# Loading the first contraction quarter of a gated FFN tile by tile, the second half of x in four transposes, and two warm-up matmuls fewer

## Chip, cores, metric

One core of a Trainium2 chip. The time of a kernel is the device time of one execution in microseconds (us); lower is better. Compared are ratios of runs made in the same rounds on the same chip. A single core's execution that is within 1.5% of the fastest of its kernel counts as fast.

## The reference

Tokens 1024, model width D = 1024, hidden width F = 3584, everything in bf16:

```python
# x (32, 32, 1024), w_gate and w_up (1024, 3584), w_down (3584, 1024)
def reference(x, w_gate, w_up, w_down):
    return (gelu_tanh(x @ w_gate) * (x @ w_up)) @ w_down
```

## The kernel before

The contraction over D runs in 8 tiles of 128 (`DT`), two to a quarter (`KQ = 2`). x is wanted with D on the partitions, so it is fetched by DMA transposes; tokens come in two halves of 512 (`NB`). F is worked through in seven chunks of 512 columns. All loads but one are issued by the sync queue, in program order. The first four F tiles (eight accumulators, gate and up of each) advance together, quarter by quarter, so that TensorE can begin before all of x is there. The cut below leaves out lines at the dots; its comments are added here.

```python
    NWARM = 9
    ...
    for _ in range(NWARM):          # matmuls on constants, so that TensorE is busy before data comes
        nc.tensor.matmul(warm_ps, lhsT=ones_w, rhs=ones_m, start=True, stop=True)
    ...
    def load_w(eng, ci, which, d0, d1):     # contraction tiles d0..d1 of chunk ci of gate (0) or up (1)
        ...
    def load_xT(t0, t1, d0, d1):
        nc.sync.dma_start_transpose(out=xT[:, d0:d1, t0:t1], in_=xf[t0:t1, d0 * P : d1 * P])
    ...
    alloc_w_chunk(0)
    load_w(nc.scalar, 0, 0, 0, KQ)
    for q in range(4):
        d0, d1 = q * KQ, (q + 1) * KQ
        load_xT(0, NB, d0, d1)
        if q > 0:
            load_w(nc.sync, 0, 0, d0, d1)
        load_w(nc.sync, 0, 1, d0, d1)
    for nb in range(1, NNB):
        load_xT(nb * NB, (nb + 1) * NB, 0, DT)
    load_w_chunk(1)
    load_wd(0)

    with tc.manual_schedule(engines={mybir.EngineType.PE}):
        head = [pair(NB) for _ in range(FC)]
        for q in range(3):
            for which in (0, 1):
                for dt in range(q * KQ, (q + 1) * KQ):
                    for ft in range(FC):
                        mm1(head[ft][which], weights_of(ft)[which], 0, NB, dt, dt + 1)
        ...                                  # last quarter, tile by tile, with the elementwise work
```

Then come the second half of the tokens for these four tiles, the other six chunks, and the second matmul with the output stores, which the sync queue issues too.

Of the kernel before, what the change touches and what calls it, by code (L numbers as in the profile page):

```python
# [16 lines left out]
def kernel(  # L17
# [8 lines left out]
    nc = tc.nc  # L26
# [9 lines left out]
    DT = D // P  # L36
# [3 lines left out]
    NB = min(N, MM_N)  # L40
# [7 lines left out]
    assert FT % FC == 0 and DT % 4 == 0  # L48
    NCH = FT // FC
    KQ = DT // 4  # L50
    NWARM = 9

    wg_r = w_gate.rearrange("(dt dp) f -> dp dt f", dp=P)
    wu_r = w_up.rearrange("(dt dp) f -> dp dt f", dp=P)
# [16 lines left out]
    warm_ps = pspool.tile([P, NB], fp32, name="warm_ps", tag="acc")  # L71
    for _ in range(NWARM):
        nc.tensor.matmul(warm_ps, lhsT=ones_w, rhs=ones_m, start=True, stop=True)  # L73
# [3 lines left out]
    def alloc_w_chunk(ci):  # L77
        w_tiles[ci] = (
            wpool.tile([P, DT, FC * P], bf16, name="wg", tag="wg"),
            wpool.tile([P, DT, FC * P], bf16, name="wu", tag="wu"),  # L80
        )

    def load_w(eng, ci, which, d0, d1):
        src = (wg_r, wu_r)[which]
        f0 = ci * FC * P
        eng.dma_start(out=w_tiles[ci][which][:, d0:d1, :], in_=src[:, d0:d1, f0 : f0 + FC * P])

    def load_w_chunk(ci):
        alloc_w_chunk(ci)
        for which in (0, 1):  # L90
            load_w(nc.sync, ci, which, 0, DT)

    def load_xT(t0, t1, d0, d1):
        nc.sync.dma_start_transpose(out=xT[:, d0:d1, t0:t1], in_=xf[t0:t1, d0 * P : d1 * P])
# [45 lines left out]
        eltwise(ft, t0, tw, *ps)  # L140

    alloc_w_chunk(0)
    load_w(nc.scalar, 0, 0, 0, KQ)
    for q in range(4):
        d0, d1 = q * KQ, (q + 1) * KQ
        load_xT(0, NB, d0, d1)
        if q > 0:
            load_w(nc.sync, 0, 0, d0, d1)
        load_w(nc.sync, 0, 1, d0, d1)
    for nb in range(1, NNB):  # L150
        load_xT(nb * NB, (nb + 1) * NB, 0, DT)
    load_w_chunk(1)
    load_wd(0)

# [38 lines left out]
    for tt in range(NT):  # L193
        tsl = slice(tt * P, (tt + 1) * P)
        for db in range(NDB):
            if tt == NT - 1 and db == NDB - 1 and DB % 2 == 0:
                q = DB // 2
# [34 lines left out]
```

## Time and profile before

| | before |
|---|---|
| time, median of 3 (range) | 301.06 us (300.96 to 301.46) |
| span of the profiled execution | 298.9 us |
| TensorE (PE) busy | 294.6 us, 99% |

From the page of the kernel before: the span, the busy line of PE with its share and number of instructions, the granted clock (the TensorE clock that the profile records as allowed) in tenths over 40 slices, and the chain of waits that ended last. PE is TensorE's matmuls, PEld its weight loads, DVE VectorE, ACT ScalarE, POOL GpSimd.

```profile
span 298.9 us, 3462 instructions
...
PE 294.6 (99%) x1381; PEld 135.4 (45%) x1381; DVE 108.2 (36%) x241; ACT 97.6 (33%) x170; POOL 0.2 (0%) x4
...
PEclk9999999999999999999999999999999999999999
...
PE 99%; DVE 0%; issue 0%
```

TensorE is the limit nearly from end to end. One thing the page does not tell: the granted clock reads full in all slices, and yet the first matmuls run at half speed. That is seen only from the starts of the matmuls one by one: 0.427 us apart at first, 0.216 us at full speed.

The timeline of the first 20 us of the kernel before (start, duration, engine; SPq and ACTq are the sync and scalar queues issuing a DMA, so their duration is issue time, not transfer time; in brackets the idle time ahead and what ended it). Merged rows of other engines and the rows between are left out.

```profile
core 0 of [0], span 298.9 us
start us, us, engine line op out<-in xcount [idle before <-releaser]
...
0.73 1.32 SPq L94 DMA_TRANSPOSE xT<-in_x_dram  x1
...
0.77 4.00 PE L73 MATMUL warm_ps<-const-bfloat16-1.0 128*128 128x512 bf16 x9 [0.77 <-PEq L216]
...
2.11 0.57 SPq L86 DMA_DIRECT2D wu<-in_w_up_dram  x1
...
4.07 0.57 SPq L86 DMA_DIRECT2D wg<-in_w_gate_dram  x1
...
4.66 2.18 PE L107 MATMUL gate_ps<-xT,wg 128*128 128x512 bf16 x8
...
8.27 1.54 PEld L107 LDWEIGHTS <-wg 128*128 128x128 bf16 x8 [0.19 <-DMA wg<-in_w_gate_dram]
8.41 1.89 PE L107 MATMUL gate_ps<-xT,wg 128*128 128x512 bf16 x8
...
10.77 5.90 SPq L94 DMA_TRANSPOSE xT<-in_x_dram  x1
...
18.87 1.19 PEld L107 LDWEIGHTS <-wg 128*128 128x128 bf16 x7 [0.43 <-DMA xT<-in_x_dram]
18.88 1.47 PE L107 MATMUL gate_ps<-xT,wg 128*128 128x512 bf16 x6
```

Nine warm-ups take 0.427 us each. The first x transpose takes 1.32 us to issue; it landed 3.9 us after its issue began, at 4.62, and the first real matmul starts at 4.66. The weight load at 8.27 waited for the second quarter's gate weights, just in time for the matmul at 8.41. The second half of x, one transpose of eight tiles, is issued from 10.77 to 16.67 and lands at 18.83, where the matmul comes 0.11 us late (the one ahead started at 18.55, and the spacing is 0.216). Loads for the next chunk wait behind it on the sync queue: the first is issued at 16.71. From 15 to 18 us, with only the 256-byte packets of this half moving, the DMA engines moved 290 GB/s; from 21 to 24 us, with plain loads, 358 GB/s.

The end of the same timeline: the last conversion to bf16, the issue of the last store, and in the header the end of the span.

```profile
core 0 of [0], span 298.9 us
...
295.42 0.42 DVE L190 CAST o_sb<-out_ps 128x256 bf16<-128x256 f32 x1 [2.63 <-PE out_ps L182]
295.87 0.33 SPq L191 DMA_DIRECT2D out_dram<-o_sb  x1
```

From 295.42 to 298.9 is the end, 3.5 us in which no matmul runs.

### The profile page before, as it was taken

The page shows a single profiled execution, that of the slowest core. Times are in us where ns is not written, and L with a number is a line of the kernel's source. Part 1 is how long each engine was busy: PE and PEld are TensorE (multiplying, and loading weights), DVE is VectorE, ACT ScalarE, POOL GpSimd, SP SyncE. Part 2 cuts the span into 40 slices and gives each one's busy share as a digit, 9 for nine tenths or more (in the row PEclk, how much of TensorE's full clock was granted, in tenths as well). Part 3 has the DMA queues.
Part 4 walks back from the last instruction along what each step waited for, and adds up shares of the span by engine and source line. Part 5 has one row for each costly group of instructions (what it writes and reads, how often), then busy time and mean ns, then how long its engine had stood idle before and what let it go on. Part 6 is the DMA issues. An engine that isn't in the chain of part 4 may idle for free.

```text
span 298.9 us, 3462 instructions
## 1 busy us (share of the span) xinstructions
PE 294.6 (99%) x1381; PEld 135.4 (45%) x1381; DVE 108.2 (36%) x241; ACT 97.6 (33%) x170; POOL 0.2 (0%) x4
## 2 busy tenths in 40 slices
PE   8999999999999999999999999999999999999995
PEld 3444444444444444444444444444444444444454
DVE  0067654455554455554445554440010001000101
ACT  1086545544544544544544544530000000000000
POOL 0000000000000000000000000000000000000000
PEclk9999999999999999999999999999999999999999
DMA  7999996080026006200800000000001000100010
GB/s 175 265 305 378 377 365 246 1 279 3 0 83 197 2 0 190 91 2 1 277 5 2 0 0 2 0 0 18 20 18 35 18 20 18 35 20 18 18 35 21
DMA packets 29168, 26.44 MB, mean 88 GB/s; under 512 B 9056, under 2 KB 25568, under 8 KB 29152
## 3 DMA queue, kind: packets, MB, share of 16 engines
q1 hardware_dynamic: 28880, 25.96, 27.8%
q10 hardware_dynamic: 272, 0.26, 0.3%
q8 instruction: 11, 0.18, 0.2%
q14 instruction: 5, 0.04, 0.1%
HBM read 22.02 MB, written 2.10 MB: 81 GB/s over the span
## 4 chain that ended last, share of the span: by engine, by line
PE 99%; DVE 0%; issue 0%
PE gate_ps L107 33%; PE out_ps L182 32%; PE up_ps L107 32%; PE warm_ps L73 1%; DVE o_sb L190 0%
## 5 line engine op out<-in xcount | busy, mean ns | idle before, releaser
L107 PE MATMUL gate_ps<-xT,wg 128*128 128x512 bf16 x448 | 106.6, 380 | 0.0
L107 PE MATMUL up_ps<-xT,wu 128*128 128x512 bf16 x448 | 106.3, 379 | 0.0
L182 PE MATMUL out_ps<-wd,gT 128*128 128x512 bf16 (+1 forms) x476 | 96.9, 366 | 0.0
L182 PEld LDWEIGHTS <-gT 128*128 128x128 bf16 x476 | 46.6, 98 | 50.4
L107 PEld LDWEIGHTS <-wg 128*128 128x128 bf16 x448 | 43.9, 98 | 53.7 <-issue 1.1
L107 PEld LDWEIGHTS <-wu 128*128 128x128 bf16 x448 | 43.8, 98 | 52.9
L117 ACT ACTIVATE h<-gate_ps 128x512 bf16<-128x512 f32 x56 | 33.4, 597 | 54.9 <-PE gate_ps L107 54.8
L125 ACT ACTIVATE s<-z 128x512 bf16<-128x512 bf16 x56 | 35.3, 630 | 45.9 <-DVE z L123 45.9
L127 DVE TENSOR_TENSOR hu<-h,up_ps 128x512 bf16<-128x512 bf16 x56 | 38.2, 682 | 16.6 <-ACT h L117 16.6
L121 DVE TENSOR_SCALAR w<-sq 128x512 bf16<-128x512 bf16 x56 | 16.4, 294 | 74.3 <-ACT sq L119 74.3
L190 DVE CAST o_sb<-out_ps 128x512 bf16<-128x512 f32 (+1 forms) x17 | 11.2, 661 | 84.6 <-PE out_ps L182 84.6
L119 ACT ACTIVATE sq<-gate_ps 128x512 bf16<-128x512 f32 x56 | 33.1, 592 | 0.0
L128 DVE TENSOR_TENSOR gT<-hu,s 128x512 bf16<-128x512 bf16 x56 | 23.8, 426 | 10.5 <-ACT s L125 10.4
L123 DVE TENSOR_TENSOR z<-w,h 128x512 bf16<-128x512 bf16 x56 | 23.8, 425 | 1.8
L73 PE MATMUL warm_ps<-const-bfloat16-1.0 128*128 128x512 bf16 x9 | 4.0, 626 | 0.8 <-PEq L216 0.8
L73 PEld LDWEIGHTS <-const-bfloat16-1.0 128*128 128x128 bf16 x9 | 1.2, 137 | 2.7 <-issue 2.7
L117 ACT ACT_TABLE_LOAD x1 | 1.3, 1283 | 1.2 <-PEq L216 1.2
L125 ACT ACT_TABLE_LOAD x1 | 1.3, 1283 | 0.0
L216 POOL MEMSET const-bfloat16-1.0<- 128x1 bf16 x1 | 0.1, 102 | 0.0
L216 POOL MEMSET const-uint8-127<- 128x1 uint8 x1 | 0.1, 102 | 0.0
L216 POOL MEMSET const-float32-0.0<- 128x1 f32 x1 | 0.1, 99 | 0.2 <-issue 0.2
L216 POOL MEMSET const-float32-1.0<- 128x1 f32 x1 | 0.1, 99 | 0.0
## 6 DMA issues: line engine op xcount, KB each, us to landing
wd<-in_w_down_dram SPq DMA_DIRECT2D x7, 1024.0 KB, 12.6
wg<-in_w_gate_dram SPq DMA_DIRECT2D x6, 1024.0 KB, 5.2
wu<-in_w_up_dram SPq DMA_DIRECT2D x6, 1024.0 KB, 7.4
out_dram<-o_sb SPq DMA_DIRECT2D x15, 128.0 KB, 1.7
wu<-in_w_up_dram SPq DMA_DIRECT2D x4, 256.0 KB, 4.7
wg<-in_w_gate_dram SPq DMA_DIRECT2D x3, 256.0 KB, 4.7
wg<-in_w_gate_dram ACTq DMA_DIRECT2D x1, 256.0 KB, 2.9
out_dram<-o_sb SPq DMA_DIRECT2D x2, 64.0 KB, 2.0
```

What stands on the lines that cost most here:

```text
L73: nc.tensor.matmul(warm_ps, lhsT=ones_w, rhs=ones_m, start=True, stop=True)
L107: nc.tensor.matmul(ps, lhsT=wt[:, dt, :], rhs=xT[:, dt, t0 : t0 + tw], start=(dt == 0), stop=(dt == DT - 1),)
L117: nc.scalar.activation(h, gate_ps, ACT.Copy)
L119: nc.scalar.activation(sq, gate_ps, ACT.Square)
L121: nc.vector.tensor_scalar(w, sq, _C2A, _C2, ALU.mult, ALU.add)
L123: nc.vector.tensor_tensor(z, w, h, ALU.mult)
L125: nc.scalar.activation(s, z, ACT.Sigmoid)
L127: nc.vector.tensor_tensor(hu, h, up_ps, ALU.mult)
L128: nc.vector.tensor_tensor(gT[:, ft, t0 : t0 + tw], hu, s, ALU.mult)
L182: nc.tensor.matmul(out_ps, lhsT=gT[:, ft, tsl], rhs=wd[:, ft, dsl], start=(ft == 0), stop=(ft == FT - 1),)
L190: nc.vector.tensor_copy(o_sb, out_ps)
L216: nc = _bacc.Bacc("TRN2", target_bir_lowering=False, num_devices=1)
```

## The change

The intent is to begin real work earlier: x and gate weights of the first quarter come in pieces of one contraction tile, so that the first tile can land sooner; with an earlier start, two warm-up matmuls can go. The second half of x comes in four pieces, so that its first tiles do not wait for its last.

```diff
-    NWARM = 9
+    NWARM = 7
...
     alloc_w_chunk(0)
-    load_w(nc.scalar, 0, 0, 0, KQ)
+    for dt in range(KQ):
+        load_w(nc.scalar, 0, 0, dt, dt + 1)
+        load_xT(0, NB, dt, dt + 1)
     for q in range(4):
         d0, d1 = q * KQ, (q + 1) * KQ
-        load_xT(0, NB, d0, d1)
+        if q > 0:
+            load_xT(0, NB, d0, d1)
         if q > 0:
             load_w(nc.sync, 0, 0, d0, d1)
         load_w(nc.sync, 0, 1, d0, d1)
     for nb in range(1, NNB):
-        load_xT(nb * NB, (nb + 1) * NB, 0, DT)
+        for q in range(4):
+            load_xT(nb * NB, (nb + 1) * NB, q * KQ, (q + 1) * KQ)
```

## The prediction

> **What bounds the kernel.** TensorE. The page has PE busy 294.6 of 298.9 us (99%), the chain of waits is 99% PE, and in it eight 512-column matmuls take 1.73 us (0.216 us each) from about 5.4 us on. 1344 full-width matmuls x 0.216 us are 290.3 us. The other 8.6 us: 0.8 us until PE starts, nine warm-up matmuls at 0.427 us, about 0.5 us because the first two or three real matmuls run at the slow clock, and the tail. Only the first 19 us can change.
>
> **The head, from the timeline.** Warm-ups end at 4.61 us. The first x transpose (issued at 0.73, issue 1.32 us, 3.9 us to landing) lands at 4.63; the first real matmul starts at 4.66. The clock is full from about 5.2 us. The second quarter's gate weights land at 8.27 us; the weight load that waited for them (0.19 us) was just in time for the matmul at 8.41: no slack. The third quarter's land at 11.45, needed 11.65. The second half of x, one transpose (issued 10.77, 8.1 us to landing), lands at 18.87; the matmul there starts 0.11 us late (18.88 after one at 18.55).
>
> **What the change does.**
> 1. Two warm-ups fewer: real work can start at 0.77 + 7 x 0.427 = 3.76. [...]Two real matmuls replace two warm-ups, worth 2 x 0.216 = 0.43 us there.
> 2. One-tile pieces: the first x tile should issue in 0.66-0.8 us (half of 1.32 plus a little) and land at 3.3-3.7 us, the half-size gate weights at about 3.1. The start at 3.76 is probably met.
> 3. One transpose instruction more on the sync queue ahead of all else: later loads issue 0.1-0.4 us later. Bytes and packets are the same. [...]the DMA share by windows, near 1 from 5 to 18 us, agrees that issuing sooner buys little.
> 4. Second half of x in four pieces: the first lands at 16-17 us, so the 0.11 us stall goes. Three more issues delay later chunk loads by tenths, with over 10 us of slack.
>
> **How much is critical.** The 0.43 us of item 1 is mostly lost: PE reaches the second quarter at about 7.9 us instead of 8.3, while its gate weights land at 8.1-8.5. Net gain there about 0.1 us (-0.2 to +0.3). Item 4 adds 0.11 us. Sum: about 0.2 us, 0.07%.
>
> **Prediction: 300.85 us, range 300.3 to 301.6.** Faster by over 2%: 0.005; within 2%: 0.985; slower by over 2%: 0.01.
>
> **What would show it right.** First real matmul at 3.7-4.0 us after 7 warm-ups, with 3-4 slow real ones; a new or longer PE wait, 0.2-0.5 us, for the second quarter's gate weights (or the first quarter's up weights at about 6 us); no wait for x at 18.9 us; span 298.3-299.3.
>
> **What would make it wrong.** If a one-tile transpose costs as much issue time as a two-tile one, later loads slip by over 1 us and the kernel is 0.5-1 us slower.[...] If the second quarter lands earlier too, the gain reaches 0.5 us.

The sum came to about 0.2 us, 0.1 us at the second quarter and 0.11 us from item 4. The 0.43 us of item 1 is the estimate: two matmuls at the 0.216 us of the trace, provided that full speed comes no later than before, which nothing had shown. For item 3 the measured values are a DMA share of 0.99 to 1.28 in each microsecond from 5 to 18 us before, and 26.44 MB in both kernels, in 29168 packets before and 29312 after; that issuing sooner buys little was an estimate from that share.

## The result, and the profile after

| | before | after |
|---|---|---|
| time, median of 6 (range) | 301.29 us (300.96 to 301.88) | 301.14 us (300.80 to 302.18) |
| ratio, 95% interval | | 0.9997 (0.9979 to 1.0015) |
| span of the profiled execution | 298.9 us | 299.1 us |
| first real matmul starts | 4.66 | 4.32 |
| second quarter starts | 8.41 | 9.18 |
| last matmul ends | 295.39 | 296.05 |
| last matmul's end to span's end | 3.47 us | 3.07 us |

A ratio is the mean time of one kernel's fast runs over that of the other's of the same rounds, so not quite the ratio of the medians quoted. The two lower rows show two differences of opposite sign: the matmuls end 0.66 us later, and what follows them is 0.40 us shorter.

The page after (some matmul records are missing from this trace, at a regular distance of 49; the weight loads are complete, 1379 = 1381 less the two warm-ups):

```profile
span 299.1 us, 3437 instructions
...
PE 293.2 (98%) x1353; PEld 135.3 (45%) x1379; DVE 108.1 (36%) x241; ACT 97.6 (33%) x170; POOL 0.2 (0%) x4
...
PE 95%; SPq 1%; DMA 1%; issue 1%; DVE 0%
```

The timeline of the first 20 us after:

```profile
core 0 of [0], span 299.1 us
...
0.73 2.54 SPq L94 DMA_TRANSPOSE xT<-in_x_dram  x2
...
0.77 3.14 PE L73 MATMUL warm_ps<-const-bfloat16-1.0 128*128 128x512 bf16 x7 [0.77 <-PEq L220]
...
3.33 0.58 SPq L86 DMA_DIRECT2D wu<-in_w_up_dram  x1
3.96 1.26 SPq L94 DMA_TRANSPOSE xT<-in_x_dram  x1
4.32 2.83 PE L107 MATMUL gate_ps<-xT,wg 128*128 128x512 bf16 x8 [0.41 <-DMA xT<-in_x_dram]
...
5.26 0.58 SPq L86 DMA_DIRECT2D wg<-in_w_gate_dram  x1
...
9.18 1.41 PEld L107 LDWEIGHTS <-wg 128*128 128x128 bf16 x8 [0.78 <-DMA wg<-in_w_gate_dram]
9.18 1.90 PE L107 MATMUL gate_ps<-xT,wg 128*128 128x512 bf16 x8 [0.29 <-DMA wg<-in_w_gate_dram]
...
19.55 0.81 PE L107 MATMUL gate_ps<-xT,wg 128*128 128x512 bf16 x3
```

Two one-tile transposes take 2.54 us to issue where one two-tile transpose took 1.32. The first tile lands at 4.28 (3.55 us after its issue began), and PE has idled 0.41 us by 4.32. Everything behind on the sync queue comes 1.2 us later: the up weights at 3.33 instead of 2.11, the second quarter's gate weights at 5.26 instead of 4.07. Those land about 9.14, and PE idles 0.29 us for them. The chain of waits (start, duration, what; gaps of about 0.05 us left out) now leads through the queue:

```profile
0.73 1.25 SPq L94
...
2.04 1.24 SPq L94
...
3.33 0.58 SPq L86
...
3.96 1.26 SPq L94
...
5.26 3.88 DMA wg<-in_w_gate_dram
...
9.18 1.90 PE gate_ps L107 x8
```

So the limit of the first 9 us has moved from TensorE to the issue of DMAs: three transposes and a weight load one after the other, then a landing. The windows from 4 to 8 us (length, then busy us and count of PE, PEld, DVE, ACT and POOL, granted clock, DMA share, GB/s) agree, before and then after:

```profile
4.00:8.00 4.00, 4.00 (x17) 1.60 (x16) 0.00 (x0) 0.00 (x0) 0.00 (x0) 1.00 1.03 233
```

```profile
4.00:8.00 4.00, 3.68 (x13) 1.48 (x13) 0.00 (x0) 0.00 (x0) 0.00 (x0) 1.00 0.82 183
```

The DMA engines did less in this stretch after the change, 183 instead of 233 GB/s: they had not yet been told what to fetch. Nor did the gate weights take longer once issued: 3.9 us to landing, before 4.2. Not contention but late issue.

The second half of x no longer holds PE: the matmul at 19.55 follows at the steady spacing. And the end of the timeline after:

```profile
core 0 of [0], span 299.1 us
...
296.09 0.42 DVE L194 CAST o_sb<-out_ps 128x256 bf16<-128x256 f32 x1 [2.63 <-PE out_ps L186]
296.54 0.33 SPq L195 DMA_DIRECT2D out_dram<-o_sb  x1
```

From the last conversion's start to the end of the span it is 3.0 us instead of 3.5, with the same conversion (0.42 us), store issue (0.33) and landing (1.6 us from issue).

### The profile page after: what moved, and what is told of

It is laid out like the page before. It is cut to its first block, busy times and chain, and to the rows that moved or that the text cites. A ratio compares the mean times of both kernels' runs of the same rounds, so it can differ in the third digit from the quotient of the medians.

```text
span 299.1 us, 3437 instructions
## 1 busy us (share of the span) xinstructions
PE 293.2 (98%) x1353; PEld 135.3 (45%) x1379; DVE 108.1 (36%) x241; ACT 97.6 (33%) x170; POOL 0.2 (0%) x4
## 2 busy tenths in 40 slices
DMA packets 29312, 26.44 MB, mean 88 GB/s; under 512 B 9200, under 2 KB 25712, under 8 KB 29296
## 4 chain that ended last, share of the span: by engine, by line
PE 95%; SPq 1%; DMA 1%; issue 1%; DVE 0%
PE out_ps L186 32%; PE up_ps L107 32%; PE gate_ps L107 32%; DMA wg<-in_w_gate_dram 1%; SPq L94 1%; SPq L86 0%; DVE o_sb L194 0%
## 5 line engine op out<-in xcount | busy, mean ns | idle before, releaser
L73 PE MATMUL warm_ps<-const-bfloat16-1.0 128*128 128x512 bf16 x7 | 3.1, 624 | 0.8 <-PEq L220 0.8
```

## The experiments

Two theories of the head (the first 19 us). *Issue theory*: a transpose costs about 1.25 us of the sync queue's time whether it brings one tile or two, so one more of them pushes all later loads back by 1.2 us, and the second quarter waits. *Clock theory*: with two warm-ups fewer and PE idle before the first real matmul, TensorE reaches its full speed later. The first four runs do each part alone, and the whole again (before: 301.34 us median of 11 on that chip).

### quarter_only: first quarter tile by tile, nothing else

```diff
# against the changed kernel
-    NWARM = 7
+    NWARM = 9
...
-        for q in range(4):
-            load_xT(nb * NB, (nb + 1) * NB, q * KQ, (q + 1) * KQ)
+        load_xT(nb * NB, (nb + 1) * NB, 0, DT)
```

> First contraction quarter tile by tile, nothing else (nine warm-ups, second half of x in one transpose). Issue theory (a transpose costs about 1.25 us of issue whether it brings one tile or two, so everything behind it on the sync queue slips 1.2 us): second quarter's gate weights issue at 5.2-5.3 us and land at about 9.2; its first matmul starts at 9.2 instead of 8.41, last matmul ends 0.7-0.9 us later than before (296.1-296.3). Clock theory (the loss in the changed kernel comes from two warm-ups fewer and the idle gap after them, which keep the clock slow for 1 us more): nine warm-ups leave no gap, full clock near 5.2 us as before, first matmul of the second quarter within 0.2 us of 8.41, last matmul end 295.2-295.6.

Measured: 301.63 us median (301.51 to 302.64), ratio 1.0010 (0.9997 to 1.0023). In the profile the two tiles issue at 0.73 and 2.02, the second quarter's gate weights at 5.25. Full speed came early, after the matmul at 4.56, so the clock theory's case of no harm was given. And still PE waited, first for up weights, then for gate weights (view of waits in the first 24 us: who, for what, total us, times, longest):

```profile
PE gate_ps L107 <- DMA wg<-in_w_gate_dram: 1.3, 1, 1.3
...
PE up_ps L107 <- DMA wu<-in_w_up_dram: 0.4, 1, 0.4
```

The second quarter began at 10.1, later than the 9.2 expected: the profiled execution was this kernel's slowest (302.64), with weights landing 4.8 us after their issue. The last matmul ended at 296.98. The issue theory holds for the direction and for the issue times; how long a landing takes varies by almost 1 us between executions (3.9 and 4.8 us for these weights in the two profiles of the changed kernel).

### warm_only: two warm-ups fewer, nothing else

```diff
# against the kernel before
-    NWARM = 9
+    NWARM = 7
```

> Two warm-ups fewer, nothing else. x still lands at 4.63, so PE is idle from about 3.8 to 4.66. Issue theory: sync queue as before, second quarter's gate weights land at about 8.3; last matmul end moves only as far as the slow clock makes PE itself late. Clock theory: full clock at about 6.3 instead of 5.3, first matmul of the second quarter at 8.9-9.2, last matmul end 0.5-0.8 us later than before. If the clock turns full at 5.3 all the same, the end is within 0.1 us of before (295.4).

Measured: 302.52 us median, ratio 1.0028 (1.0006 to 1.0051); five executions at 302.25 to 302.78 and one at 300.45. The timeline shows why (the sync queue issues the second quarter's gate weights at 4.25 as it should):

```profile
4.25 0.58 SPq L86 DMA_DIRECT2D wg<-in_w_gate_dram  x1
4.83 3.57 PE L107 MATMUL gate_ps<-xT,wg 128*128 128x512 bf16 x8 [0.92 <-DMA xT<-in_x_dram]
...
8.20 2.06 PE L107 MATMUL up_ps<-xT,wu 128*128 128x512 bf16 x8
```

x lands at 4.79, PE has idled 0.92 us, and then eight matmuls take 3.57 us, all at the slow spacing, and the next begins so too. Full speed (the first matmul that the next one follows at 0.216 us) comes at 8.6. The clock theory is right about this kernel. One execution in six was 2 us faster; it was not profiled, so that full speed came earlier there is likely and not shown. So both costs exist, and here the two removed warm-ups were affordable only where x came earlier, which is what the tile-by-tile load is for.

### half_only: second half of x in four pieces, nothing else

```diff
# against the kernel before
-        load_xT(nb * NB, (nb + 1) * NB, 0, DT)
+        for q in range(4):
+            load_xT(nb * NB, (nb + 1) * NB, q * KQ, (q + 1) * KQ)
```

> Second half of x in four transposes, nothing else. Both theories: head as before up to 18.5 us, no wait for x there, first matmul of the second half 0.11 us earlier (18.77 instead of 18.88), last matmul end about 295.28, time 0.1 us lower (0.9996), not to be told from noise by the time alone. First piece lands at 15.5-17 us. The next chunk's loads issue within 0.5 us of before or 1-2 us later if each transpose has a fixed cost[...]; no PE wait either way.

Measured: 301.21 us median, ratio 1.0002 (0.9989 to 1.0015). The first piece landed at 15.8, and no matmul waited for x. The last matmul ended at 295.75, not at 295.28: in this execution full speed came at 6.1 instead of before's 5.4 and the whole head was 0.5 us late already at the second quarter. This shows how little one pair of profiles can tell: five profiles of kernels whose head is that of the kernel before up to 10 us (before, half_only, pad4, pad5, half_pad) have full speed at 5.4, 6.1, 3.6, 3.6 and 6.8 us and the last matmul's end at 295.39, 295.75, 295.23, 295.63 and 296.02.

### after_again: the changed kernel once more

No edit.

> The changed kernel once more, for a narrower ratio and a second profile. Issue theory: second quarter's gate weights again land near 9.2 and PE waits there, last matmul end 295.9-296.2; the point where the clock turns full may move without moving the end. Clock theory: the end follows the point where the clock turns full. Time ratio 1.000-1.003.

Measured: 300.93 us median (300.75 to 301.93), ratio 0.9987 (0.9974 to 1.0000). The profiled execution was again the slowest (301.93): the gate weights, issued at 5.25, landed at 10.03, the last matmul ended at 296.95. Both profiles of this kernel have a later head than before's, and yet the times are not higher (the other four executions here: 300.75 to 301.07). The parts do not add up either: alone they cost 0.10%, 0.28% and 0.02% (only the 0.28% is clear of zero); together they cost nothing and may gain. Something outside the head was missing, or the parts interact. The next four runs tested the interaction (before: 301.02 us median of 11 on that chip).

### nine_warm: the changed kernel with nine warm-ups

```diff
# against the changed kernel
-    NWARM = 7
+    NWARM = 9
```

> The changed kernel with nine warm-ups again (first quarter tile by tile and second half in four pieces stay). What is asked: why first quarter tile by tile alone was 0.1% slower than before, and the whole change 0.13% faster. If the two warm-ups are what pays (two more real matmuls done before the second quarter), this kernel is 0.2-0.7 us slower than the changed one measured in the call before (300.93 of a before at 301.34), so ratio 1.000-1.001. If the four pieces are what pays, because the slipped sync queue would bring an unsplit second half too late, this kernel is as fast as the changed one, ratio 0.998-0.9995: PE waits at the second quarter anyway, so the two warm-ups there only lengthen a wait. In the trace the second quarter starts when its gate weights land (9.1-10.1), with a shorter wait than with seven warm-ups.

Measured: 300.98 us median, ratio 0.9995 (0.9983 to 1.0007). The second quarter began at 8.98 when its weights landed. By its ratio it is not to be told from the changed kernel (0.9997 and 0.9987, on other chips): no gain from the two warm-ups fewer is to be seen. The trace fits: PE waits at the second quarter (0.6 us) either way.

### no_half: the changed kernel with the second half of x in one transpose

```diff
# against the changed kernel
-        for q in range(4):
-            load_xT(nb * NB, (nb + 1) * NB, q * KQ, (q + 1) * KQ)
+        load_xT(nb * NB, (nb + 1) * NB, 0, DT)
```

> The changed kernel with the second half of x in one transpose again (first quarter tile by tile and seven warm-ups stay). If the four pieces pay: ratio 1.000-1.002, and in an execution whose second quarter starts near 9.2, PE waits 0.3-0.9 us at about 19.4-20 us for the second half of x, issued near 11.5-12.4 and landing 8 us later. If the warm-ups pay: ratio 0.998-0.9995, and no such wait over 0.15 us.

Measured: 301.55 us median (301.52 to 301.65), ratio 1.0016 (1.0003 to 1.0029). By the time alone "the four pieces pay" would have been confirmed. But the profile has no wait for the second half of x at all, its second quarter starts at 9.17 and its last matmul ends at 296.04, as in the changed kernel (9.18 and 296.05). Its span is longer by 0.5 us, all of it after the last matmul: 3.60 us instead of 3.07. The expected reason was wrong, and the end of the program came into view.

### one_transpose: the changed kernel with x of the first quarter in one transpose

```diff
# against the changed kernel
     for dt in range(KQ):
         load_w(nc.scalar, 0, 0, dt, dt + 1)
-        load_xT(0, NB, dt, dt + 1)
+    load_xT(0, NB, 0, KQ)
```

> The changed kernel with x of the first quarter in one two-tile transpose again (gate weights in two pieces, seven warm-ups, four pieces stay). Issue theory: one transpose less ahead of everything, so the second quarter's gate weights issue at about 4.2 and land at 8.3-8.7 and PE does not wait for them. But x lands at 4.6-4.9, so PE idles about 1 us after the warm-ups as in the run with two warm-ups fewer alone, where the full clock came at 8.6 and the median was 302.5. Clock theory: median 302-302.7, ratio 1.002-1.005, full clock after 8 us in the profile. If only the sync queue mattered: ratio 0.998-0.9995.

Measured: 303.16 us median, ratio 1.0066 (1.0054 to 1.0078).

```profile
4.04 0.58 SPq L86 DMA_DIRECT2D wg<-in_w_gate_dram  x1
...
5.68 3.57 PE L107 MATMUL gate_ps<-xT,wg 128*128 128x512 bf16 x8 [1.77 <-DMA xT<-in_x_dram]
```

Taking the one extra transpose out moves the second quarter's gate weights back from 5.26 to 4.04: the issue theory's 1.2 us, undone by one edit. But x landed only at 5.6, 4.9 us after its issue began; PE idled 1.77 us and reached full speed at 9.7. So the late start and the slow clock cost more than the queue here, in the direction expected and beyond the size. The number of warm-ups is the same as in the changed kernel, whose two profiles with an idle gap of 0.41 and 0.60 us reach full speed at 6.3 and 6.2 us.

### two_queues: weights of the first chunk issued by the scalar queue

```diff
# against the changed kernel
-    NWARM = 7
+    NWARM = 8
...
         if q > 0:
-            load_w(nc.sync, 0, 0, d0, d1)
-        load_w(nc.sync, 0, 1, d0, d1)
+            load_w(nc.scalar, 0, 0, d0, d1)
+        load_w(nc.scalar, 0, 1, d0, d1)
```

> An improvement that the issue theory points to: the changed kernel with eight warm-ups and all first-chunk weights issued on the scalar queue, only the transposes on sync. The sync queue then issues the second quarter's x at 3.3-4.6 and the scalar queue the second quarter's gate weights at 2.1-2.6, landing by 7.5. Issue theory: no PE wait at the second quarter or later, the first x tile lands at 4.3 or, if the other weights share the engines with it, up to 0.5 later; last matmul end 295.0-295.5; ratio 0.997-0.999. If the shared engines and not the issue order hold the second quarter back: its weights land at 8.5-9.2 all the same and the ratio is 0.999-1.001.

Measured: 303.89 us median (302.88 to 305.46), ratio 1.0099 (1.0074 to 1.0125): a failed improvement, outside both expectations. (Its three slowest executions show a mean granted clock of 0.989 to 0.994; the profiled one, at 303.27 us, 1.0.)

```profile
2.02 9.59 SPq L94 DMA_TRANSPOSE xT<-in_x_dram  x5
...
8.18 1.02 PE L107 MATMUL gate_ps<-xT,wg 128*128 128x512 bf16 x4 [2.14 <-DMA xT<-in_x_dram]
```

The second x tile, issued at 2.02 (2.04 in the changed kernel), took 6.1 us to land instead of 2.8. From 3 to 4 us, 229 of the 1 KB weight packets from the other queue started and no 256-byte packet of x. PE stood still for 2.14 us. Issuing early was no gain here, where data that was not yet needed went ahead of data that was.

### The end of the program

Ten profiles were now there. The raw records of the sync queue have, in seven of them, a pause of 0.42 to 0.45 us (no recorded instruction starts) between the 79th and the 80th recorded instruction of that queue, wherever these fall, with no wait seen that explains it. In the other three (after, after_again, nine_warm) this same place is taken by the wait for the last store, 1.12 to 1.14 us. Before, the pause is between two drains (DRAIN, one of the instructions that close the program) after the last store has landed:

```text
kernel before, sync queue: start  end (us)  instruction
295.874 296.206  DMA issue, last store (the 73rd)
...
296.442 297.454  semaphore wait: last store landed
297.521 297.549  semaphore wait
297.601 297.614  drain (the 79th)
298.068 298.184  drain
```

```text
changed kernel, sync queue: start  end (us)  instruction
296.539 296.872  DMA issue, last store (the 77th)
296.917 296.934  semaphore wait
296.976 297.004  semaphore wait (the 79th)
298.140 298.168  semaphore wait: last store landed (298.123)
```

The changed kernel has four transposes more on this queue (9 instead of 5). The 79th is now a semaphore wait just ahead of the one for the last store, so that a pause there would pass while that wait goes on anyway. At which of the closing waits the last store is awaited also went with the number of DMAs (numbers below the table of all profiles). Theory: the shorter end is worth 0.4 to 0.5 us, and has nothing to do with what was loaded. The last four runs tested this by adding or removing sync DMAs behind the head (they issue at about 37 to 44 us, and their data is first used at 198 us; the head ends at 19) (before: 301.27 us median of 11 on that chip).

### pad5: the kernel before, five more sync DMAs, late

```diff
# against the kernel before
+    WD_CUTS = {5: (0, 1, 2, 4), 6: (0, 1, 2, 3, 4)}
+
     def load_wd(ci):
-        fsl = slice(ci * FC, (ci + 1) * FC)
-        nc.sync.dma_start(out=wd[:, fsl, :], in_=wd_r[:, fsl, :])
+        cuts = WD_CUTS.get(ci, (0, FC))
+        for lo, hi in zip(cuts, cuts[1:]):
+            fsl = slice(ci * FC + lo, ci * FC + hi)
+            nc.sync.dma_start(out=wd[:, fsl, :], in_=wd_r[:, fsl, :])
```

> The kernel before with five more loads on the sync queue late in the program (two w_down loads of 1 MB cut in three and in four pieces, needed 50 us later), head untouched. End theory, formed from ten profiles: in each the sync sequencer pauses 0.42-0.45 us between its 79th and 80th recorded instruction, wherever those fall; in the kernel before that is after the last output landed (last matmul end to end of span 3.47 us), in the changed kernel it coincides with the wait for that landing (3.07 us). With five more, the 79th is ahead of that wait, so the pause hides: last matmul end to span end 3.0-3.1 us, time 0.3-0.5 us lower than before, ratio 0.998-0.999. Rival (the end depends on nothing in the sync stream; the shorter end of the changed kernel is chance or comes from its head): 3.4-3.6 us and ratio 0.9995-1.0005.

Measured: 300.74 us median (300.54 to 300.84), ratio 0.9982 (0.9969 to 0.9995). Last matmul's end to span's end 3.04 us. The end of its timeline:

```profile
core 0 of [0], span 298.7 us
...
295.67 0.42 DVE L194 CAST o_sb<-out_ps 128x256 bf16<-128x256 f32 x1 [2.63 <-PE out_ps L186]
296.12 0.33 SPq L195 DMA_DIRECT2D out_dram<-o_sb  x1
```

### pad4: control, four more sync DMAs

```diff
# against pad5
-    WD_CUTS = {5: (0, 1, 2, 4), 6: (0, 1, 2, 3, 4)}
+    WD_CUTS = {5: (0, 2, 4), 6: (0, 1, 2, 3, 4)}
```

> Control for the run with five: four more loads instead (w_down loads cut in two and in four). End theory: the pause after the 79th recorded sync instruction falls after the wait for the last output (which is the 79th itself), so it shows: last matmul end to span end 3.4-3.6 us, ratio to before 0.9995-1.0005. If cutting the w_down loads as such made the kernel faster, this one is as fast as the one with five.

Measured: 301.27 us median, ratio 1.0001 (0.9989 to 1.0013). Last matmul's end to span's end 3.54 us.

```profile
core 0 of [0], span 298.8 us
...
295.27 0.42 DVE L194 CAST o_sb<-out_ps 128x256 bf16<-128x256 f32 x1 [2.63 <-PE out_ps L186]
295.72 0.33 SPq L195 DMA_DIRECT2D out_dram<-o_sb  x1
```

From the last conversion's start to the span's end it is 3.0 us with five more and 3.5 with four. One DMA more or less, behind the head and long ahead of the end, moves the time by 0.53 us (the five executions of each do not overlap), about as expected before the runs. That smaller w_down loads as such make it faster is ruled out by this pair.

### after_minus1: the changed kernel, one sync DMA less, late

```diff
# against the changed kernel
-    def load_wd(ci):
-        fsl = slice(ci * FC, (ci + 1) * FC)
+    def load_wd(ci, n=1):
+        fsl = slice(ci * FC, (ci + n) * FC)
...
-        load_wd(ci)
+        if ci < NCH - 2:
+            load_wd(ci)
+        elif ci == NCH - 1:
+            load_wd(ci - 1, 2)
```

> The changed kernel with one sync instruction less late in the program (the last two w_down loads as one), head untouched. End theory: the pause shows again, last matmul end to span end 3.4-3.6 us instead of 3.07, time 0.3-0.5 us above the changed kernel, so ratio to before 1.0005-1.002: what the changed head is worth with the same end is a loss of 0.1-0.6 us. Rival: 3.0-3.1 us, ratio 0.9985-0.9997 as in the earlier runs of the changed kernel.

Measured: 301.71 us median (301.43 to 302.68), ratio 1.0022 (1.0008 to 1.0037). The end is 3.55 us long again:

```profile
296.82 0.42 DVE L197 CAST o_sb<-out_ps 128x256 bf16<-128x256 f32 x1 [2.63 <-PE out_ps L189]
297.27 0.33 SPq L198 DMA_DIRECT2D out_dram<-o_sb  x1
```

The span ends at 300.3. With the pause visible in both kernels, the changed head is slower than the old one, clear of noise: 0.44 us by the medians, 0.66 by the ratio (0.24 to 1.1), of which 0.08 is the end (3.55 instead of 3.47). The merged w_down load, the only other difference, lands at 53 us and is first read at 200 us.

### half_pad: the old head, four pieces for the second half of x, and a hidden pause

```diff
# against half_only; load_wd takes WD_CUTS as in pad5
+    WD_CUTS = {5: (0, 2, 4), 6: (0, 2, 4)}
```

> Version meant to beat both: the kernel before, with the second half of x in four pieces, and two w_down loads cut in two each (five more sync instructions in all), nine warm-ups, first quarter as before. End theory: pause hidden, 3.0-3.1 us from last matmul end to span end; no wait for the second half of x; time 0.3-0.6 us lower than before, ratio 0.998-0.999, and not slower than the changed kernel (0.9987 and 0.9997 of before so far). Rival: as the run with the four pieces alone, ratio 0.9995-1.0005.

Measured: 300.56 us median (300.51 to 301.12), ratio 0.9984 (0.9972 to 0.9996), end 3.03 us. The lowest median, clear of the kernel before, but not to be told from pad5 (0.9982). Against the changed kernel there is no run on the same chip; its two ratios to before are 0.9997 and 0.9987, with intervals that overlap this one.

All profiles together (number of recorded sync instructions; place of the last store's issue among them; last matmul's end to span's end):

| kernel | sync instructions | last store | end, us |
|---|---|---|---|
| before, warm_only | 83 | 73rd | 3.47, 3.47 |
| quarter_only, no_half | 84 | 74th | 3.60, 3.60 |
| half_only, one_transpose, after_minus1 | 86 | 76th | 3.56, 3.54, 3.55 |
| pad4 | 87 | 77th | 3.54 |
| after, after_again, nine_warm | 87 | 77th | 3.07, 3.06, 3.04 |
| pad5, half_pad | 88 | 78th | 3.04, 3.03 |
| two_queues | 80 | 70th | 3.07 |

pad4 and the changed kernel have the same counts on the sync queue and differ in the closing wait at which the last store is awaited (the changed kernel has one more DMA on the scalar queue, and which wait it is goes with the number of all DMAs: with 51, 52, 53 and 54 of them the last store's semaphore is number 102, 103, 104 and 105): in pad4 ahead of the pause, in the changed kernel behind it. In two_queues the 79th is the last but one of 80, past all that, and the end is 3.07 us.

## Why the prediction was right or wrong

The number was right: 300.85 us predicted with a range of 300.3 to 301.6, measured 301.14. The way there was partly wrong, and two errors cancelled: that is luck. With the old end, the changed head would have come to about 301.73 (an estimate: 301.29 and the 0.44 us of after_minus1), outside the range.

1. *What bounds the kernel, and that only tenths are to be had*: right. All variants of the changed kernel's parts lie within 1% of before.
2. *"The first x tile should issue in 0.66-0.8 us (half of 1.32 plus a little) and land at 3.3-3.7 us"*: wrong. It issued in 1.25 us and landed at 4.28. The error was to scale issue time by tiles from one size; the trace before had no one-tile transpose, and it could not tell a fixed cost from one per tile. So the start at 3.76 was not met (4.32), and the 0.43 us of item 1 shrank to 0.34 us of earlier start.
3. *"Later loads issue 0.1-0.4 us later"*: the failed step. It was 1.19 us (gate weights of the second quarter 5.26 instead of 4.07), shown in every kernel with two one-tile transposes and these weights on the sync queue (5.25 to 5.26) and undone in one_transpose (4.04). The prediction had named this under what would make it wrong, with 0.5 to 1 us of loss; the profile's last matmul is 0.66 us late and after_minus1, with an end like before's, loses 0.44 us by the medians.
4. *"PE reaches the second quarter and waits for its gate weights"*: right as a mechanism, with weights at 9.14 instead of 8.1 to 8.5. *"Net gain there about 0.1 us"*: wrong in sign, a loss of 0.77 us in this pair of profiles, 0.44 us by the times of after_minus1.
5. *The four pieces end the 0.11 us stall*: right in the trace (landing at 16.7, no wait), too small for the times (half_only 1.0002).
6. *A gap after the seventh warm-up can delay full speed*: the risk is real, and large where x came in one piece: gaps of 0.92 and 1.77 us, full speed at 8.6 and 9.7 us (warm_only, one_transpose). Where x came tile by tile after seven warm-ups, full speed came at 6.2 to 6.5 us (after, after_again, after_minus1) and in no_half, whose head is the same up to there, at 4.5; PE waited at the second quarter in all four.
7. *"Only the first 19 us can change"*: wrong. The end of the program is missing from the prediction. Added DMAs on the sync queue moved a pause of 0.43 to 0.45 us under a wait. It is worth 0.53 us (pad5 against pad4) and gives back what the head loses. Shown by pad5, pad4 and after_minus1, in both directions.

Sum, by the medians: head +0.44 us, end -0.53 us, together about -0.1; measured -0.15 and, in the second set, -0.41, with intervals that include -0.1. By the ratios it is +0.66 and -0.57, together +0.1. The two shares are shown; the sign of their sum is not.

What stays open: what the pause is. It sits between the 79th and the 80th recorded instruction of the sync queue, for 0.42 to 0.45 us. The traces show one thing more near it: in all 14 profiles an 8 KB DMA packet of the kind "instruction" starts 1.06 to 1.35 us after the end of the 79th, wherever that falls (at 298.70 before, 297.81 in pad5, 301.90 in two_queues). But it starts 0.18 us or more after the 80th has begun, so it is not what the pause waits for: the cause of the pause is not shown. Open too is why landings of one kernel differ by almost 1 us between executions.

## What to carry to other kernels

Cutting a transpose in two did not halve its issue time here: 1.24 to 1.25 us for one tile (after, quarter_only), 1.23 to 1.53 for two in the first 7 us (before, after, quarter_only, warm_only, half_only, one_transpose), 5.90 for eight (before). At 1.25 us each, the sync queue in the head of this kernel is a budget: one more transpose on it delayed everything behind by 1.2 us, needed or not. Where a change is worth tenths of a microsecond, follow it to the very end of the span, and put the same number of DMAs on the queue in the control: otherwise a gain or loss can come from where the instructions happen to fall (0.53 us here, pad5 against pad4). Before warm-ups are removed, see when the first real operand lands: an idle gap of 0.92 us after them was followed by nine matmuls at half speed in warm_only, and its median is 1.2 us higher.
